# Expert stages of an attention and MoE kernel: a w2 remainder behind the group's end, two terms of a down tile amid the next, and another order of the next expert's preparation

## The chip, the cores and the metric

The kernel runs on one core of a Trainium2 chip. Its time is the device time of one execution in microseconds (us); the median of three runs of the kernel before is 734.19 us (733.92 to 736.5). The profile is that of one more execution, which took 734.46 us.

## The reference

The program computes causal attention with a decay for 8 batches of 8 heads, 576 rows and 64 values a head, and sends the result, as 4608 rows of 512 values, through a mixture of 8 experts with one expert a row:

```python
logits = x @ w_gate
expert_idx = np.argmax(logits, axis=1)
...
for e in range(E):
    mask = expert_idx == e
    xe = x[mask]
    h = np.maximum(xe @ w1[e], 0.0)
    ye = h @ w2[e]
    out[mask] = gate_w[mask, None] * ye
```

Here `w1[e]` is 512 x 1024 and `w2[e]` is 1024 x 512. The attention is not touched by the change.

## The kernel before

The attention and expert 0 take the first half of the span. From expert 1 on (the loop in `run` over `e`), each expert has an **up stage** and a **down stage**.

Every float32 factor is held as two parts: a high part, which ScalarE makes by a cast (`round_s`, `round_v`'s predecessor `split_v`, `split_t`), and a low part, the **remainder**, which VectorE or GpSimd makes as the factor less its high part. A product is then three matmuls: high by high, high by low, low by high.

**Up stage** (`sevens`, `group`, `product`). The expert's up to 640 rows are paired into 320 columns, and the product with w1 is done by Strassen's scheme: four groups of seven block products, 42 matmuls a group, 168 in all. A register picks one of three widths (320, 288 or 256 columns). The sums of input blocks are called T1 to T4; the unsummed input lies in `xa` and `B22`. The weight sums are made by GpSimd in four additions (`sums_s`, lines 1386 to 1389). After certain products ScalarE, VectorE and GpSimd combine the results (`after`, lines 1546 to 1569) and make h = Relu(...) in a high part `hh` (line 1538) and a low part `hl` (line 1541). GpSimd has one addition in it, `p5` (line 1560). The last steps of a group, `end`, a Relu and `last`, run amid the next group, and those of the last group at the head of the down stage (`self.ends`).

**Down stage** (`downs`, `down`). Five tiles of 128 rows, each the sum over eight hidden blocks of three matmuls (24 in all) with 512 columns into one PSUM bank. The blocks go in the order

```python
        terms = [(ft, *i) for ft in ((0, 1, 2, 4, 5, 6, 3, 7) if e else range(FT))
```

since blocks 3 and 7 come from the last group. Tiles 0, 2 and 4 use one PSUM bank, tiles 1 and 3 another. ScalarE then scales the tile into `y` (line 1293), and GpSimd scatters its rows into the output (line 1296). All of the fifth tile but its first matmul is skipped where an expert has few rows (`tail`).

**Weights.** w2 comes in four blocks `i` of two hidden blocks; block 3 holds hidden blocks 6 and 7. `split_v` casts a block (ScalarE, line 1416) and makes its remainder (VectorE, line 1417). w1 comes in four groups of two parts (`part` 0 of 128x1024 elements, `part` 1 of 128x768); line 1401 is the cast, line 1407 the remainder.

**Preparation of the next expert.** GpSimd gathers the rows of five input tiles (`fetch`), SP writes them to memory and reads them back in another order (`put`, `get`), VectorE transposes them into PSUM (`flip`, line 1178), and ScalarE and VectorE make the input sums from there (`turn_t`: copies at lines 1470 to 1472, six subtractions or additions at lines 1469 and 1476). `split_t` splits a finished sum T1 to T4 into its two parts (lines 1416 and 1417 again).

**What sets the order.** Two tables written by hand: `ups` says which preparation is issued after which of the 28 products (k = 0 to 27), `dns` which after which quarter of the first four down tiles (k = 0 to 15; four quarters a tile, two hidden blocks each). `InOrder.pin` ties every instruction to the one before it on its engine, so that the order of issue is the order in each engine's queue and in the DMA queues of SP and GpSimd. An engine whose next instruction waits holds up all behind it.

Of the kernel before, what the change touches and what calls it, by code (L numbers as in the profile page):

```python
# [9 lines left out]
F32 = mybir.dt.float32  # L10
# [5 lines left out]
ALU = mybir.AluOpType  # L16
# [6 lines left out]
S = 576  # L23
# [10 lines left out]
NST = CAP // P  # L34
# [4 lines left out]
FT = FF // P  # L39
# [1033 lines left out]
class Moe:  # L1073
# [185 lines left out]
    def down(self, e, m, part=(0, FT)):  # L1259

        c, nc = self.c, self.nc
        rows = self.rows_of_h(e, m)
        if part[0] == 0:
            self.py[m] = psum((c.ps_v, c.ps_m)[m % 2])
        py = self.py[m]
        terms = [(ft, *i) for ft in ((0, 1, 2, 4, 5, 6, 3, 7) if e else range(FT))
                 for i in ((0, 0), (0, 1), (1, 0))]

        def some(k0, k1):
            for k in range(k0, k1):  # L1270
                ft, hi_, wi = terms[k]
                c.note(nc.tensor.matmul(  # L1272
                    py, rows(hi_, ft), self.w2p[e, ft][wi],
                    start=k == 0, stop=k == len(terms) - 1, skip_group_check=tail,
                ))

        tail = e > 0 and m == NST - 1
        if tail:
            some(0, 1)
            few = self.tail  # L1280
            if e + 1 < E:
                self.begin_up(e + 1)
            else:
                self.tc.mark_branch_hint_location("overflow", engines=[mybir.EngineType.PE])
            with self.tc.If(few > 0):
                some(1, len(terms))
        else:
            some(3 * part[0], 3 * part[1])
        if part[1] < FT:
            return  # L1290
        _, si, g, s = self.index(e, m)
        y = c.yp.tile([P, D], F32, name="y")
        nc.scalar.activation(y, py, AF.Copy, scale=g[:, s : s + 1])  # L1293

        def scatter():
            nc.gpsimd.indirect_dma_start(  # L1296
                out=self.out,
                out_offset=bass.IndirectOffsetOnAxis(ap=si[:, s : s + 1], axis=0),
                in_=y, in_offset=None, bounds_check=self.x_dram.shape[0] - 1,
                oob_is_err=False,  # L1300
            )

        if tail and e + 1 < E:
            self.scatter = scatter
        else:
            scatter()
# [123 lines left out]

    def split_v(self, e, i):

        c = self.c
        hi, lo = (self.w2_part(c.words, i, k) for k in range(2))
        self.round(hi, lo, self.w2_part(c.values, i, 1))
        for f in range(2):
            self.w2p[e, 2 * i + f] = [w[:, f * D : f * D + D] for w in (hi, lo)]

# [164 lines left out]
    def run(self, run, tasks):  # L1603
        c, tc = self.c, self.tc
        T = lambda f, *args: lambda: f(*args)
# [3 lines left out]
        def downs(e, ms, tasks):  # L1609
            k = 0  # L1610
            for m in ms:
                for q in range(4):
                    if e and m == NST - 1:
                        if q == 0:
                            run(lambda: self.down(e, m))
                    else:
                        run(lambda: self.down(e, m, (2 * q, 2 * q + 2)))
                    for f in tasks.get(k, []):
                        run(f)
                    k += 1  # L1620

        with tc.tile_pool(name="moe_w2b", bufs=1, side="right") as w2b:
# [4 lines left out]
            S = lambda f, *args: T(f, 1, *args)  # L1627
# [20 lines left out]
        with tc.tile_pool(name="moe_h", bufs=1) as hp, tc.tile_pool(name="moe_u", bufs=1) as up_, \  # L1648
# [5 lines left out]
            for e in range(1, E):  # L1654
                self.h[e] = h
                if e == 1:
                    run(lambda: self.begin_up(e))
                S = lambda f, *args: T(f, e, *args)
                N = lambda f, *args: T(f, e + 1, *args)
                ups, dns = {}, {}  # L1660

                def at(d, *items):
                    for k, f in items:
                        d.setdefault(k, []).append(f)

                late = 9 if e == 1 else 1
                at(ups, (0, S(self.load_v, 0)), (0, S(self.load_v, 1)),
                   (4, S(self.round_s, 2, 1)), (6, S(self.rest_s, 2, 1, G)),
                   (late, S(self.load_v, 2)), (late, S(self.load_v, 3)),
                   (9 if e > 1 else 8, S(self.split_s, 3, 0)), (11, S(self.round_s, 3, 1)),  # L1670
                   (13, S(self.rest_s, 3, 1, G)))
                for i, k in enumerate((15, 22, 16, 23) if e == 1 else (10, 23, 16, 24)):
                    at(ups, (k, S(self.split_v, i)))
                if e == 1:
                    at(ups, (0, S(self.sums_s, 3)), (2, S(self.split_s, 2, 0)))
                else:
                    at(ups, (8, self.scatter))
                if e + 1 < E:
                    at(ups, (9, N(self.load_s, 0)), (16, N(self.load_s, 1)),
                       (6, fetch(e + 1, 3)), (6, fetch(e + 1, 4)), (13, fetch(e + 1, 2)),  # L1680
                       (15, fetch(e + 1, 0)), (19, fetch(e + 1, 1)), (20, N(self.sums_s, 0)),
                       (27, N(self.sums_s, 1)))
                    for m, i, k in ((3, 12, 16), (4, 13, 17), (2, 18, 22), (0, 21, 26), (1, 25, 27)):
                        at(ups, (i, N(self.put, m)), (k, N(self.get, m)))
                    at(dns, (0, N(self.begin_t)), (1, N(self.round_s, 0, 0)),
                       (2, N(self.round_s, 0, 1)), (5, N(self.flip, 3)), (5, N(self.flip, 4)),
                       (6, N(self.rest_s, 0, 0)), (6, N(self.turn_t, 3)),
                       (7, N(self.rest_s, 0, 1)), (7, N(self.load_s, 2)),
                       (7, N(self.turn_t, 4)), (9, N(self.flip, 2)), (9, N(self.split_s, 1, 0)),
                       (10, N(self.turn_t, 2)), (11, N(self.flip, 0)),  # L1690
                       (11, N(self.split_s, 1, 1)), (11, N(self.load_s, 3)),
                       (12, N(self.sums_s, 2)), (13, N(self.turn_t, 0)),
                       (14, N(self.flip, 1)), (15, N(self.turn_t, 1)),
                       (15, N(self.split_t, "T2")), (15, N(self.split_t, "T1")),
                       (15, N(self.split_t, "T4", G)), (15, N(self.split_t, "T3", G)),
                       (15, N(self.split_s, 2, 0)), (15, N(self.sums_s, 3)))
                else:
                    at(ups, (27, lambda: tc.keep_in_program_order(G.drain())))
                self.ends = [lambda: None] * 3
                self.sevens(e, run, ups)  # L1700
                dns.setdefault(0, [])[:0] = self.ends
                downs(e, range(NST), dns)


# [224 lines left out]
```

## Time and profile before

| what | value |
|---|---|
| median of 3 runs | 734.19 us (733.92 to 736.5) |
| the profiled execution | 734.46 us |
| its span, first to last instruction | 732.7 us |
| TensorE busy (matmuls) | 719.4 us, 98% |
| VectorE busy | 559.2 us, 76% |
| GpSimd busy | 549.5 us, 75% |
| ScalarE busy | 496.7 us, 68% |
| mean granted TensorE clock | 0.986 of full speed |

The profile names TensorE's matmuls PE, its weight loads PEld, VectorE DVE, ScalarE ACT, GpSimd POOL and SyncE SP. A row names line, engine, operation and tile. "Idle before" is the time for which the engine stood idle ahead of an instruction, with what ended the wait. The end of a matmul is modelled, so the pace of TensorE is read from start to start. Times in the rows are counted from the start of the span.

### The profile page before, as it was taken

The numbers are of one execution on the slowest core, as the hardware profiler recorded it, in microseconds if no ns is written. First come the engines' busy times: TensorE is split into PE (matmuls) and PEld (weight loads), VectorE is DVE, ScalarE is ACT, GpSimd is POOL, SyncE is SP. The second block draws the span as 40 slices with busy tenths as digits, with TensorE's granted clock in tenths as the row PEclk, the third lists the DMA queues.
The fourth block names the chain that finished last, engine by engine and source line by source line (L and its number), as shares of the span: only waits on it lengthen the run. The fifth ranks groups of instructions, "written<-read, shape, count | busy, mean of one in ns | idle before, by whom it ended". The sixth has DMA issues, their size and how long they took to land.

```text
span 732.7 us, 18458 instructions
## 1 busy us (share of the span) xinstructions
PE 719.4 (98%) x6321; PEld 620.6 (85%) x6321; DVE 559.2 (76%) x1614; ACT 496.7 (68%) x1319; POOL 549.5 (75%) x696
## 2 busy tenths in 40 slices
PE   9999999999999999999999999999999999999997
PEld 4888888888888888798898898897898887998985
DVE  6678898989898988671979777798698697796830
ACT  6999999999999999352665555574565664755631
POOL 5999989898989888945687497595794794884711
PEclk8999999999999999899999999999999999999999
DMA  6886788867776756324357376384574574673301
GB/s 181 210 193 178 193 208 205 211 187 219 194 212 192 214 190 226 109 95 132 112 191 239 123 235 202 118 262 154 187 208 147 170 230 133 194 220 99 126 22 42
DMA packets 98724, 127.59 MB, mean 174 GB/s; under 512 B 10287, under 2 KB 56367, under 8 KB 98608
## 3 DMA queue, kind: packets, MB, share of 16 engines
q1 hardware_dynamic: 91568, 106.12, 49.4%
q0 software_dynamic: 6400, 19.93, 8.3%
q8 instruction: 71, 1.16, 0.7%
q14 instruction: 45, 0.37, 0.2%
q10 hardware_dynamic: 640, 0.01, 0.0%
HBM read 99.12 MB, written 27.93 MB: 173 GB/s over the span
## 4 chain that ended last, share of the span: by engine, by line
PE 75%; POOL 11%; issue 5%; DVE 4%; DMA 4%; ACT 1%; POOLq 0%; DVEq 0%; ACTq 0%
PE ps L1272 24%; PE ps L1492 12%; PE ps L526 11%; PE ps L403 9%; PE ps L455 7%; PE ps L437 4%; PE ps L1227 3%; PE ps L450 2%; POOL w L1090 1%; POOL xg L1156 1%; DMA bias<-ud 1%; PE ps L617 1%; POOL w1r L1387 1%; PE pr L1492 1%; POOL X_1w L1417 1%
## 5 line engine op out<-in xcount | busy, mean ns | idle before, releaser
L422 ACT ACTIVATE sc<-sc,nmx 128x512 f32<-128x512 f32 (+3 forms) x256 | 142.3, 558 | 5.3 <-DVE nmx L379 4.1
L1296 POOL DMA_INDIRECT out<-y,si_fast x40 | 44.2, 1105 | 90.5 <-ACT y L1293 73.5
L1272 PE MATMUL ps<-w_0w,hhw 128*128 128x512 f32 x273 | 106.5, 390 | 2.1 <-ACT hhw L1538 2.1
L1492 PE MATMUL ps<-X_0w,w1s 128*128 128x320 f32 (+2 forms) x504 | 107.6, 304 | 0.0
L1272 PE MATMUL ps<-w_0w,hl 128*128 128x512 f32 x272 | 107.5, 395 | 0.0
L1272 PE MATMUL ps<-w_1w,hhw 128*128 128x512 f32 x272 | 106.7, 392 | 0.0
L467 ACT COPY aT<-ps 128x512 f32<-128x512 f32 (+1 forms) x224 | 93.3, 506 | 1.3 <-PE ps L455 0.3
L330 POOL TENSOR_TENSOR hl<-raw,hl 128x640 fp32r<-128x640 f32 (+1 forms) x60 | 89.6, 1493 | 5.0
L526 PE MATMUL ps<-aT,va_t 128*64 128x256 f32 (+3 forms) x896 | 90.6, 354 | 0.0
L1293 ACT ACTIVATE y<-ps,g_fast 128x512 f32<-128x512 f32 x40 | 27.5, 687 | 85.5 <-PE ps L1272 62.7
L1492 PEld LDWEIGHTS ps<-X_0w,w1s 128*128 128x128 f32 x504 | 83.1, 190 | 0.1
L526 PEld LDWEIGHTS ps<-aT,va_t 128*64 128x64 f32 x896 | 56.4, 137 | 28.7 <-issue 5.4
L403 PE MATMUL ps<-hl 64*128 64x512 f32 (+1 forms) x720 | 80.5, 340 | 0.0
L1492 PE MATMUL ps<-X_1w,w1s 128*128 128x320 f32 (+2 forms) x252 | 76.2, 302 | 0.0
L379 DVE CUSTOM_DVE_ANT_0 sc<-ps,bias 128x128 f32<-128x128 f32 (+1 forms) x128 | 59.8, 486 | 10.1 <-PE ps L403 4.6
L1272 PEld LDWEIGHTS ps<-w_0w,hhw 128*128 128x128 f32 x273 | 51.3, 188 | 14.3 <-ACT hhw L1538 3.4
L1272 PEld LDWEIGHTS ps<-w_1w,hhw 128*128 128x128 f32 x272 | 51.1, 188 | 11.5
L1272 PEld LDWEIGHTS ps<-w_0w,hl 128*128 128x128 f32 x272 | 51.1, 188 | 11.2 <-DVE hl L1541 0.9
L379 DVE CUSTOM_DVE_ANT_1 sc<-ps,bias 128x256 f32<-128x256 f32 (+1 forms) x128 | 57.7, 487 | 3.6 <-PE ps L403 3.5
L1492 PE MATMUL ps<-xa,w1s 128*128 128x320 f32 (+2 forms) x336 | 56.8, 304 | 3.4 <-ACT xa L1472 1.2
L1407 DVE TENSOR_TENSOR w1s<-w1r,w1s 128x1024 fp32r<-128x1024 f32 (+1 forms) x42 | 49.6, 1183 | 10.8 <-ACT w1s L1401 10.7
L403 PEld LDWEIGHTS ps<-hl 64*128 64x128 f32 x720 | 52.4, 185 | 3.3
(252 smaller groups left out, 1896.5 us busy)
## 6 DMA issues: line engine op xcount, KB each, us to landing
bias<-ud SPq DMA_DIRECT2D x30, 576.0 KB, 5.8
w1r<-in_w SPq DMA_DIRECT2D x112, 128.0 KB, 2.6
w<-in_w SPq DMA_DIRECT2D x28, 512.0 KB, 5.5
raw<-in_qkT SPq DMA_DIRECT2D x64, 160.0 KB, 3.4
raw<-in_qkT SPq DMA_DIRECT2D x64, 144.0 KB, 3.7
va_t<-in_va SPq DMA_DIRECT2D x32, 256.0 KB, 5.7
x_dram<-row SPq DMA_DIRECT2D x32, 256.0 KB, 2.7
xs<-xg SPq DMA_DIRECT2D x30, 256.0 KB, 3.6
```

What stands on the lines that cost most here:

```text
L330: return eng.tensor_tensor(hl[:, 1], raws[n][:, r : r + w], hl[:, 0].bitcast(F32), ALU.subtract)
L379: red_last[:] = [V.tensor_tensor_reduce(dst, src, in1, -0.125, init, ALU.add, ALU.min, nms[n][:, col : col + 1]).ins]
L403: note(nc.tensor.matmul(pb[j][:, o : o + w], q[js], k[js], start=(i == 0), stop=(i == len(terms) - 1),))
L422: A.activation(x, x, AF.Exp, bias=nms[n][:, 5 * j + t : 5 * j + t + 1], scale=-1.0, accum_out=ssums[b][:, t, 2 * p + j : 2 * p + j + 1])
L437: note(nc.tensor.matmul(pb[half][:, 0:JW], q, k, start=(i == 0), stop=(i == len(terms) - 1),))
L455: note(nc.tensor.transpose(out.bitcast(F32R), words, c.identr[rows, rows]))
L467: copy_on = {"a": lambda o, i: A.copy(o, i), "v": lambda o, i: V.tensor_copy(o, i)}
L526: note(nc.tensor.matmul(pv[j * HD : (j + 1) * HD, q0 - qa : qb - qa], l, r, start=(blk == 0), stop=(blk == nb - 1),))
L1272: c.note(nc.tensor.matmul(py, rows(hi_, ft), self.w2p[e, ft][wi], start=k == 0, stop=k == len(terms) - 1, skip_group_check=tail,))
L1296: nc.gpsimd.indirect_dma_start(out=self.out, out_offset=bass.IndirectOffsetOnAxis(ap=si[:, s : s + 1], axis=0), in_=y, in_offset=None, bou ...
L1407: (eng or self.nc.vector).tensor_tensor(lo, raw, hi.bitcast(F32), ALU.subtract)
L1492: self.nc.tensor.matmul(bank[:, 0:cols], w[:, wi, mat, kt], x[xi][:, kt, 0:cols], start=start and k == 0, stop=k == 5, skip_group_check=True,)
```

## The change

Four edits, all in experts 1 to 7.

1. `split_v` is cut into `round_v` (the cast) and `rest_v` (the remainder). For w2 block 3 the cast stays after product 23 or 24, and the remainder goes behind the three last steps of the last product group, at the head of the down stage.
2. In the first down tile (`head`), the two terms that use that remainder, (6, 0, 1) and (7, 0, 1), are sorted to the end, held back, and issued by `finish_down` after the first quarter of the second tile, with the tile's scaling and scatter (now `down_out`) behind them.
3. In `dns` the casts, transposes, input tiles and splits of the next expert stand at other quarters, most of them earlier: the last input tile is turned at 10 instead of 15, the sums T1 to T4 are split at 12 and 14 instead of 15.
4. The remainders of both parts of w1 group 0 and of part 1 of group 1 go from VectorE to GpSimd (argument `G`); those of T3 and T4 go from GpSimd to VectorE.

```diff
--- before.py
+++ after.py
@@ -1265,16 +1265,18 @@
         py = self.py[m]
         terms = [(ft, *i) for ft in ((0, 1, 2, 4, 5, 6, 3, 7) if e else range(FT))
                  for i in ((0, 0), (0, 1), (1, 0))]
+        tail, head = (e > 0 and m == t for t in (NST - 1, 0))
+        if head:
+            terms.sort(key=lambda t: t in ((6, 0, 1), (7, 0, 1)))
 
         def some(k0, k1):
             for k in range(k0, k1):
                 ft, hi_, wi = terms[k]
                 c.note(nc.tensor.matmul(
                     py, rows(hi_, ft), self.w2p[e, ft][wi],
-                    start=k == 0, stop=k == len(terms) - 1, skip_group_check=tail,
+                    start=k == 0, stop=k == len(terms) - 1, skip_group_check=tail or head,
                 ))
 
-        tail = e > 0 and m == NST - 1
         if tail:
             some(0, 1)
             few = self.tail
@@ -1285,9 +1287,17 @@
             with self.tc.If(few > 0):
                 some(1, len(terms))
         else:
-            some(3 * part[0], 3 * part[1])
+            some(3 * part[0], 3 * part[1] - (2 if head and part[1] == FT else 0))
         if part[1] < FT:
             return
+        if head:
+            self.finish_down = lambda: (some(len(terms) - 2, len(terms)), self.down_out(e, m, py, tail))
+        else:
+            self.down_out(e, m, py, tail)
+
+    def down_out(self, e, m, py, tail):
+
+        c, nc = self.c, self.nc
         _, si, g, s = self.index(e, m)
         y = c.yp.tile([P, D], F32, name="y")
         nc.scalar.activation(y, py, AF.Copy, scale=g[:, s : s + 1])
@@ -1430,9 +1440,20 @@
 
     def split_v(self, e, i):
 
+        self.round_v(e, i)
+        self.rest_v(i)
+
+    def rest_v(self, i):
+
+        hi, lo = (self.w2_part(self.c.words, i, k) for k in range(2))
+        self.nc.vector.tensor_tensor(lo, self.w2_part(self.c.values, i, 1), hi.bitcast(F32),
+                                     ALU.subtract)
+
+    def round_v(self, e, i):
+
         c = self.c
         hi, lo = (self.w2_part(c.words, i, k) for k in range(2))
-        self.round(hi, lo, self.w2_part(c.values, i, 1))
+        self.nc.scalar.copy(hi, self.w2_part(c.values, i, 1))
         for f in range(2):
             self.w2p[e, 2 * i + f] = [w[:, f * D : f * D + D] for w in (hi, lo)]
 
@@ -1615,6 +1636,8 @@
                             run(lambda: self.down(e, m))
                     else:
                         run(lambda: self.down(e, m, (2 * q, 2 * q + 2)))
+                        if e and (m, q) == (1, 0):
+                            run(self.finish_down)
                     for f in tasks.get(k, []):
                         run(f)
                     k += 1
@@ -1669,8 +1692,9 @@
                    (late, S(self.load_v, 2)), (late, S(self.load_v, 3)),
                    (9 if e > 1 else 8, S(self.split_s, 3, 0)), (11, S(self.round_s, 3, 1)),
                    (13, S(self.rest_s, 3, 1, G)))
-                for i, k in enumerate((15, 22, 16, 23) if e == 1 else (10, 23, 16, 24)):
+                for i, k in enumerate((15, 22, 16) if e == 1 else (10, 23, 16)):
                     at(ups, (k, S(self.split_v, i)))
+                at(ups, (23 if e == 1 else 24, S(self.round_v, 3)))
                 if e == 1:
                     at(ups, (0, S(self.sums_s, 3)), (2, S(self.split_s, 2, 0)))
                 else:
@@ -1683,22 +1707,23 @@
                     for m, i, k in ((3, 12, 16), (4, 13, 17), (2, 18, 22), (0, 21, 26), (1, 25, 27)):
                         at(ups, (i, N(self.put, m)), (k, N(self.get, m)))
                     at(dns, (0, N(self.begin_t)), (1, N(self.round_s, 0, 0)),
-                       (2, N(self.round_s, 0, 1)), (5, N(self.flip, 3)), (5, N(self.flip, 4)),
-                       (6, N(self.rest_s, 0, 0)), (6, N(self.turn_t, 3)),
-                       (7, N(self.rest_s, 0, 1)), (7, N(self.load_s, 2)),
-                       (7, N(self.turn_t, 4)), (9, N(self.flip, 2)), (9, N(self.split_s, 1, 0)),
-                       (10, N(self.turn_t, 2)), (11, N(self.flip, 0)),
-                       (11, N(self.split_s, 1, 1)), (11, N(self.load_s, 3)),
-                       (12, N(self.sums_s, 2)), (13, N(self.turn_t, 0)),
-                       (14, N(self.flip, 1)), (15, N(self.turn_t, 1)),
-                       (15, N(self.split_t, "T2")), (15, N(self.split_t, "T1")),
-                       (15, N(self.split_t, "T4", G)), (15, N(self.split_t, "T3", G)),
-                       (15, N(self.split_s, 2, 0)), (15, N(self.sums_s, 3)))
+                       (1, N(self.round_s, 0, 1)), (2, N(self.flip, 3)), (2, N(self.flip, 4)),
+                       (2, N(self.turn_t, 3)), (2, N(self.turn_t, 4)),
+                       (2, N(self.rest_s, 0, 0, G)), (2, N(self.rest_s, 0, 1, G)),
+                       (6, N(self.flip, 2)), (6, N(self.flip, 0)), (6, N(self.turn_t, 2)),
+                       (7, N(self.turn_t, 0)), (7, N(self.load_s, 2)),
+                       (7, N(self.split_s, 1, 0)), (8, N(self.round_s, 1, 1)),
+                       (8, N(self.rest_s, 1, 1, G)), (8, N(self.flip, 1)),
+                       (10, N(self.turn_t, 1)), (11, N(self.load_s, 3)),
+                       (12, N(self.split_t, "T2")), (12, N(self.split_t, "T1")),
+                       (12, N(self.sums_s, 2)), (14, N(self.split_t, "T4")),
+                       (14, N(self.split_t, "T3")), (15, N(self.split_s, 2, 0)),
+                       (15, N(self.sums_s, 3)))
                 else:
                     at(ups, (27, lambda: tc.keep_in_program_order(G.drain())))
                 self.ends = [lambda: None] * 3
                 self.sevens(e, run, ups)
-                dns.setdefault(0, [])[:0] = self.ends
+                dns.setdefault(0, [])[:0] = [*self.ends, T(self.rest_v, 3)]
                 downs(e, range(NST), dns)
```

## Rows read from the trace of the kernel before

**Rows 1.** By stage: us, busy PE, PEld, DVE, ACT, POOL (instructions); clock, DMA, GB/s.

```profile
391.85:420.05 28.20, 27.94 (x122) 22.39 (x121) 22.43 (x49) 13.60 (x31) 15.96 (x17) 1.00 0.49 158
420.05:444.69 24.64, 24.64 (x169) 24.64 (x168) 18.54 (x31) 15.50 (x30) 23.05 (x20) 1.00 0.76 244
444.69:472.19 27.50, 27.50 (x123) 22.55 (x122) 22.07 (x49) 13.61 (x31) 14.79 (x16) 1.00 0.39 128
...
494.64:523.26 28.62, 27.92 (x123) 22.38 (x121) 22.87 (x50) 13.93 (x32) 16.38 (x17) 1.00 0.43 135
...
597.22:622.37 25.15, 22.82 (x100) 17.88 (x98) 20.25 (x43) 11.34 (x28) 15.26 (x16) 1.00 0.53 165
622.37:649.80 27.43, 26.41 (x168) 26.15 (x169) 22.51 (x39) 18.76 (x34) 23.52 (x21) 0.94 0.71 218
```

**Rows 2.** Waits of TensorE, 367 to 727 us: us, times, longest.

```profile
PE ps L1272 <- ACT hhw L1538: 2.1, 3, 1.1
...
PE ps L1492 <- ACT w1s L1401: 1.1, 1, 1.1
```

**Rows 3.** Timeline of TensorE, expert 5, tile 0: start, us, what, idle before.

```profile
601.11 0.40 PE L1272 MATMUL ps<-w_0w,hl 128*128 128x512 f32 x1
602.64 0.50 PE L1272 MATMUL ps<-w_0w,hhw 128*128 128x512 f32 x1 [1.13 <-ACT hhw L1538]
```

**Rows 4.** Timeline of the other engines, 596.6 to 604.6 us, expert 5.

```profile
596.69 2.91 DVE L1417 TENSOR_TENSOR w_1w<-w,w_0w 128x1024 fp32r<-128x1024 f32 x2
...
598.48 1.72 POOL L1388 TENSOR_TENSOR w1r<-w1r 128x256 f32<-128x256 f32 x1
600.17 0.73 POOL L1389 TENSOR_TENSOR w1r<-w1r 128x256 f32<-128x256 f32 x1
...
600.86 0.87 POOL L1560 TENSOR_TENSOR u<-u,u 128x320 f32<-128x320 f32 x1
...
602.16 0.43 ACT L1538 ACTIVATE hhw<-ps 128x320 fp32r<-128x320 f32 x1
...
602.71 0.48 DVE L1541 SCALAR_TENSOR_TENSOR hl<-ps,hhw 128x320 fp32r<-128x320 f32 x1
```

**Rows 5.** Timeline of TensorE, expert 5 to expert 6.

```profile
620.78 0.39 PE L1272 MATMUL ps<-w_0w,hhw 128*128 128x512 f32 x1
622.37 0.56 PE L1492 MATMUL ps<-xa,w1s 128*128 128x320 f32 x2 [1.20 <-ACT xa L1472]
623.94 1.44 PE L1492 MATMUL ps<-xa,w1s 128*128 128x320 f32 x4 [1.01 <-DVE xa L1469]
```

**Rows 6.** Timeline of ScalarE and VectorE at the same place.

```profile
619.77 1.09 DVE L1178 STREAM_TRANSPOSE ps<-xg 128x512 f32<-128x512 f32 x1
...
621.03 0.69 ACT L1293 ACTIVATE y<-ps,g_fast 128x512 f32<-128x512 f32 x1 [2.86 <-issue]
...
621.61 0.26 ACT L1470 COPY X<-ps 128x128 f32<-128x128 f32 x1
...
622.35 0.29 DVE L1469 TENSOR_TENSOR X<-ps,X 128x128 f32<-128x128 f32 x1 [1.48 <-ACT xa L1472]
...
623.47 0.42 DVE L1469 TENSOR_TENSOR xa<-ps,xa 128x256 fp32r<-128x256 f32 x1
```

**Rows 7.** Groups by shape on VectorE, 391.85 to 677.3 us: busy us, mean ns.

```profile
L1407 DVE TENSOR_TENSOR w1s<-w1r,w1s 128x1024 fp32r<-128x1024 f32 x22 | 26.7, 1215 | 7.7 <-ACT w1s L1401 7.7
...
L1417 DVE TENSOR_TENSOR X_1w<-X,X_0w 128x640 fp32r<-128x640 f32 x12 | 9.4, 822 | 0.8
```

**Rows 8.** Groups by shape on GpSimd, the same stretch.

```profile
L1417 POOL TENSOR_TENSOR X_1w<-X,X_0w 128x640 fp32r<-128x640 f32 x11 | 22.7, 2078 | 14.1 <-ACT X_0w L1416 14.1
...
L1407 POOL TENSOR_TENSOR w1s<-w1r,w1s 128x768 fp32r<-128x768 f32 x10 | 18.7, 1866 | 0.0
```

**Rows 9.** SP's last reads back, expert 5; DMA issues, 590:612, us to landing.

```profile
602.34 3.07 SPq L1171 DMA_DIRECT2D xg<-xs  x2
...
xg<-xs SPq DMA_DIRECT2D x5, 256.0 KB, 4.2
```

## The prediction

> **What bounds the kernel now.** First the page: TensorE is busy for nearly the whole span and the matmuls are the same before and after, so only time in which TensorE waits or runs slowly can be won, and only from the first expert's end on, where the edits lie. Second, a table by stage, one stretch per up or down stage [rows 1]. An undisturbed down stage of five tiles (120 matmuls) takes 27.50 us, 0.229 us a matmul and 5.50 us a tile. The same work takes 28.20 us in expert 1 and 28.62 us in expert 3: 0.70 and 1.12 us over. Expert 5 skips its fifth tile after one matmul (97 in all), which should be 97 x 0.229 = 22.23 us, and takes 25.15: 2.92 over. The up stage behind it, of full width as the undisturbed one of 24.64 us, takes 27.43: 2.79 over, at a mean granted clock of 0.94 where the other five have 1.00. These four sums, 7.53 us or 1.0% of the span, are all that the edits aim at.
>
> Third, who ended the waits: a Relu on ScalarE in the down stage (2.1 us in three places), and one wait of 1.1 us in the middle of expert 5's up stage, put down to a ScalarE cast [rows 2]. I leave that last one as it is: the work that it is put down to keeps its place in the change.
>
> **The stall inside tile 0.** The down products go through the 1024 hidden columns in the order 0, 1, 2, 4, 5, 6, 3, 7, because blocks 3 and 7 come from the last product group. In expert 5 the first matmul of block 3 starts at 602.64 us where the pace gives 601.11 + 0.23 = 601.34: 1.30 us late [rows 3]. It needs the Relu that ends at 602.16 + 0.43 = 602.59. Walk back [rows 4]: that Relu stands behind another which waited for a GpSimd addition (600.86 to 601.73), which stood behind GpSimd's four weight sums. The third of these took 1.72 us, the fourth 0.73. Beside the third VectorE was making the remainders of two w2 blocks, 2.91 us for the pair, where a remainder of 128x1024 has a mean of 1.22 elsewhere [rows 7]: each engine holds up the other. VectorE's own part of that addition also stood behind the pair.
>
> **The change, part by part.**
> *Last w2 remainder behind the group's end.* One 128x1024 subtraction leaves this place in each of seven experts. The VectorE chain comes forward by 2.91 - 1.22 = 1.7 us. GpSimd's third sum should fall from 1.72 to about 0.73, so its addition ends 0.99 earlier, at 600.74. GpSimd is the later of the two, so the gain is 0.99, not 1.7. The two Relus then end at 602.59 - 0.99 = 601.60.
> *Two terms of tile 0 put last.* Block 6's remainder term leaves the place ahead of block 3, so block 3 is wanted one matmul earlier, at 601.11 in expert 5. What is left there: 601.65 - 601.11 = 0.54 us, and the smaller delays behind it (1.56 in all less 1.30 = 0.26, where 1.56 is 2.92 less the 1.36 before the next stage, below): 0.80. By the same shift (-0.99 + 0.23 = -0.76) expert 3 keeps some 0.36 of its 1.12 and expert 1 nothing of its 0.70. I round expert 3's rest down to 0.2, since part of its 1.12 are the small delays after the stall. So 0.70 + 1.12 + 1.56 = 3.38 us becomes 1.0: **2.4 us won**. Bounds: 0 (the sums don't get shorter) and 3.38.
> *The deferred terms themselves.* They run after 28 other matmuls, 28 x 0.229 = 6.4 us into the stage, at 603.6 + 0.8 = 604.4 in expert 5. VectorE's last remainder of the group now ends at 602.71 + 0.48 = 603.19 [rows 4], then at 602.20; the w2 remainder behind it takes 1.22 to 1.7 and is there by 603.9. No stall; cover 0.5 us.
> *Tile 0's output later.* Its ScalarE evacuation (0.69 us, [rows 6]) now waits for 30 matmuls, and stands behind the copies of two input tiles, which wait for two VectorE transposes (1.09 each) behind the w2 remainder: 603.9 + 2.2 + 0.7 (copies, 621.61 to 622.35) + 0.7 = 607.5. Its PSUM bank is wanted by tile 2 at 597.22 + 0.8 + 48 x 0.229 = 609.0. Spare 1.5 us; cost nothing. Its scatter queues behind GpSimd's remainders, and its buffer is wanted again only by tile 2's output.
> *GpSimd makes three remainders.* One of 128x1024 and two of 128x768 per expert: 1.87 us each for the small [rows 8], an estimated 1.87 x 1024/768 = 2.5 for the large, 6.2 in all. It gives up two 128x640 remainders of 2.08. VectorE loses 3.2 us and gains 2 x 0.82. None of these is wanted by TensorE before the next up stage, 20 us on. SP's loads of the third weight group wait for the first two remainders: GpSimd is through its four sums at 600.74 + 4 x 0.73 = 603.7 and with both remainders at 608.1; before, VectorE had them behind transposes and an input tile at 603.19 + 2 x 1.09 + 1.22 = 606.6 and, 1.54 and some 1 later, 609.1. That queue is no later. The bounds are 0 and what the second rival says.
> *Input tiles earlier.* This is the other large term. In expert 5 TensorE goes from its last down matmul at 620.78 to the first up matmul at 622.37, then waits again until 623.94 [rows 5]: the last input tile is transposed only at 619.77, and its copies stand on ScalarE behind tile 3's output at 621.03, which ends with that tile; the low part of the input is there at 623.89 [rows 6]. Everywhere else the fifth tile covers this. In the new order ScalarE copies the last input tile before tile 2's output. VectorE's queue from 603.9: two transposes, two tiles of six subtractions (1.54 each, 622.35 to 623.89), two transposes, two tiles, one weight remainder, transpose, tile: 603.9 + 5 x 1.09 + 5 x 1.54 + 1.22 = 618.3. The re-read rows were issued by 605.41 and take 4.2 us to land [rows 9], so they are there before their transposes. The splits of the four input sums follow, a cast and a remainder of 0.82 [rows 7] each: the first by 618.3 + 2 x 0.82 = 619.9, the fourth by 622.4. The up products start at 620.2 and come 24.64/28 = 0.88 us apart, and the second, third, fourth and sixth want these sums: 621.1 to 624.6. In time by 1.2 us or more.
> So 1.59 - 0.23 = 1.36 us goes before the stage, and its 2.79 over: 4.15. In that 2.79 are 1.2 us of the second wait and some 1.5 of a clock at the lower level: 0.94 over 27.43 us is 0.06/0.5 x 27.43 = 3.3 us at 1.2 instead of 2.4 GHz, and it came right after these two waits; the waits of 1.1 to 1.3 us elsewhere brought no lower clock. What stays is the jump over the skipped tile, which no other stage shows: between 0 and 1.36; I take 0.3, as a stage change without a jump shows none. **3.85 us won**.
> *Sum.* The profiled execution took 734.46 us (span 732.7 and 1.8 around it), 0.27 above the median of 734.19. 734.46 - 2.4 - 3.85 = 728.2, less 0.27: **727.9 us**, 0.86% faster.
>
> **A rule of the Trainium skill.** [Rows 4] show the two engines lengthening each other. "SBUF — State Buffer", section "SBUF: two separate sides", says why: a VectorE instruction with two SBUF inputs and a GpSimd instruction exclude each other for the whole instruction, it is a lock and no sharing. The pair at 2.91 and the sum at 1.72 agree with it. By that rule the longer GpSimd remainders speak against this change: each may hold a VectorE remainder for its whole length. The third rival below is that outcome.
>
> **Rivals.**
> 1. *Only the input tiles help.* GpSimd's sums stay long, because the remaining w2 remainder and the chain before them set their end; tile 0 stalls as now or by 0.23 more in three experts. For: GpSimd has hardly a gap through the up stage. Against: the fourth sum, with no remainder beside it, took 0.73. Time: 734.46 - 3.85 + 0.5 - 0.27 = 730.8; if half comes through, 729.6. Chance 0.13.
> 2. *Only tile 0 helps.* The splits of the input sums run beside GpSimd's sums for the third group and take up to twice as long, or the jump and tile 4's output cost as much as the wait now does. For: the margins of little over 1 us above. Against: the first products want only the input itself. Time: 734.46 - 2.4 - 0.27 = 731.8. Chance 0.15.
> 3. *Slower: tile 0's output blocks tile 2.* If a GpSimd remainder gets ahead of VectorE's w2 remainder, it holds that, and behind it the transposes, the copies and the evacuation at 607.5, by up to 2.5 us, or 4.4 with the second. Six experts pay what exceeds 1.5 us: with 4.4 it is 6 x 2.9 = 17 us, 745; it turns to a loss from 6.25/6 = 1.04 us beyond the spare, a hold of 2.5. Against: GpSimd's sums last until 603.7 and the w2 remainder asks at 602.2. Chance 0.07.
> 4. *It does neither*, since another wait takes over in both places: 734.2, chance 0.05.
>
> **Chances.** The forecast has 0.60, with its own range from 726.6 (all 7.53 won) to 729.5. This kernel can tell about 0.5%, 3.7 us, from no change: faster is below 730.5, which takes the forecast, half of rival 1 and a little of 2, where the first wait goes whole: 0.70. The same has 0.21: the rest of 1 and 2, and 4. Slower has 0.09: rival 3 and something not seen. The range goes from 725.8 (with the wait of 1.1 us in expert 5's up stage gone too) to 732.2, which takes in rivals 1 and 2.
>
> **What would show it.** Right: expert 3's and 5's first block 3 matmul late by under 0.6 us; the third sum before it near 0.73; no gap over 0.5 us between expert 5's last down and first up matmul, and a granted clock of 1.00 in that up stage; tile 0's evacuation done by 10.5 us into the stage. Wrong: a wait of TensorE at a tile 2, at the deferred terms, or for an input sum's split; GpSimd's sums still at 1.7.

## The result and the profile after

The changed kernel took 726.88 us (median of six runs, 725.69 to 728.06), the kernel before 733.87 us in the same rounds (six runs, 731.74 to 736.5): a ratio of 0.9912 [0.9893, 0.9932]. The forecast was 727.9 us, a ratio of 0.9914. The profiled execution took 727.32 us with a span of 725.5, against 734.46 and 732.7 before.

The table by stage again, from the first product of a stage to the first of the next. Columns as in [rows 1]; the rows are expert 1's, 2's, 3's and 5's down stage and the up stage behind expert 5.

```profile
390.87:418.37 27.50, 27.50 (x122) 22.50 (x121) 23.20 (x49) 14.20 (x31) 22.18 (x19) 1.00 0.52 153
...
443.01:470.51 27.50, 27.50 (x122) 22.54 (x121) 23.30 (x48) 14.19 (x31) 23.01 (x20) 1.00 0.39 126
492.97:520.82 27.85, 27.85 (x122) 22.38 (x121) 23.44 (x50) 14.50 (x32) 23.28 (x19) 1.00 0.40 125
594.05:617.85 23.80, 22.84 (x99) 17.89 (x98) 21.41 (x48) 14.00 (x32) 19.02 (x16) 1.00 0.56 178
617.85:642.60 24.75, 24.75 (x169) 24.74 (x169) 21.03 (x33) 16.23 (x31) 22.98 (x21) 1.00 0.72 221
```

Beside [rows 1], expert 1 lost the whole of its 0.70 us, expert 3 kept 0.35 of 1.12, expert 5 kept 1.57 of 2.92, and the up stage behind it came down from 27.43 to 24.75 at a full granted clock. POOL's busy time in these down stages rose by 3.8 to 8.2 us: it has the remainders now. Two of TensorE's four waits from 360 us to the end matter here (us in total, times, longest); the Relu's three waits of [rows 2] are one, and the second is the jump over the skipped tile. The other two, of 0.4 and 0.3 us, lie in the up stages of experts 1 and 5:

```profile
PE ps L1275 <- ACT hhw L1559: 0.6, 1, 0.6
...
PE ps L1513 <- PEq L1287: 0.3, 1, 0.3
```

TensorE at the two places of [rows 3] and [rows 5], in expert 5 (start, us, what, idle before): block 3's first product, and the step to expert 6.

```profile
597.52 0.39 PE L1275 MATMUL ps<-w_0w,hhw 128*128 128x512 f32 x1
...
598.79 0.50 PE L1275 MATMUL ps<-w_0w,hhw 128*128 128x512 f32 x1 [0.64 <-ACT hhw L1559]
...
617.14 0.39 PE L1275 MATMUL ps<-w_0w,hhw 128*128 128x512 f32 x1
617.85 0.84 PE L1513 MATMUL ps<-xa,w1s 128*128 128x320 f32 x4 [0.32 <-PEq L1287]
```

Tile 0 now waits at 597.52 + 2 x 0.23 = 597.98 and goes on at 598.79: 0.81 us instead of 1.30. The step to the next expert has 617.85 - 617.14 = 0.71 us between two starts that are 0.23 apart elsewhere: 0.48 lost, and no second wait. GpSimd around tile 0:

```profile
595.62 0.74 POOL L1398 TENSOR_TENSOR w1r<-w1r 128x256 f32<-128x256 f32 x1
596.32 0.74 POOL L1399 TENSOR_TENSOR w1r<-w1r 128x256 f32<-128x256 f32 x1
597.01 0.87 POOL L1581 TENSOR_TENSOR u<-u,u 128x320 f32<-128x320 f32 x1
...
599.50 1.73 POOL L1398 TENSOR_TENSOR w1r<-w1r 128x256 f32<-128x256 f32 x1
...
601.88 4.22 POOL L1417 TENSOR_TENSOR w1s<-w1r,w1s 128x1024 fp32r<-128x1024 f32 x2
```

The third sum of the old group takes 0.74 us instead of the 1.72 of [rows 4]; the same instruction of the next group (599.50) takes 1.73, because the moved w2 remainder (599.25, below) now lies beside it, where no product waits for the sum. ScalarE and VectorE in the same stage:

```profile
598.31 0.42 ACT L1559 ACTIVATE hhw<-ps 128x320 fp32r<-128x320 f32 x1
...
603.25 0.72 ACT L1303 ACTIVATE y<-ps,g_fast 128x512 f32<-128x512 f32 x1
...
612.85 0.39 ACT L1493 CAST xa<-ps 128x256 fp32r<-128x256 f32 x1
613.12 0.71 ACT L1303 ACTIVATE y<-ps,g_fast 128x512 f32<-128x512 f32 x1
```

```profile
599.25 1.37 DVE L1449 TENSOR_TENSOR w_1w<-w,w_0w 128x1024 fp32r<-128x1024 f32 x1
...
614.40 0.42 DVE L1490 TENSOR_TENSOR xa<-ps,xa 128x256 fp32r<-128x256 f32 x1
614.95 4.44 DVE L1427 TENSOR_TENSOR X_1w<-X,X_0w 128x640 fp32r<-128x640 f32 x4
```

Tile 0's output leaves at 603.97, 9.9 us into the stage. The last input tile's copies stand ahead of tile 2's output. Its low part is there at 614.82, 20.8 us into the stage instead of 26.7 (623.89 in [rows 6]), and VectorE's splits of the input sums begin 2.9 us before the next stage's first product.

### The profile page after: what moved, and what is told of

Its sections match the earlier page's. It is cut to its first block, busy times and chain, and to the rows that moved or that the text cites. A ratio compares the mean times of both kernels' runs of the same rounds, so it can differ in the third digit from the quotient of the medians.

```text
span 725.5 us, 18440 instructions
## 1 busy us (share of the span) xinstructions
PE 715.7 (99%) x6321; PEld 617.2 (85%) x6321; DVE 555.9 (77%) x1608; ACT 497.9 (69%) x1319; POOL 573.7 (79%) x702
## 5 line engine op out<-in xcount | busy, mean ns | idle before, releaser
L1306 POOL DMA_INDIRECT out<-y,si_fast x40 | 48.1, 1202 | 59.5 <-ACT y L1303 27.9
L1417 POOL TENSOR_TENSOR w1s<-w1r,w1s 128x768 fp32r<-128x768 f32 (+1 forms) x32 | 62.8, 1968 | 0.1
```

The lines of the kernel that those rows point to most:

```text
L1306: nc.gpsimd.indirect_dma_start(out=self.out, out_offset=bass.IndirectOffsetOnAxis(ap=si[:, s : s + 1], axis=0), in_=y, in_offset=None, bou ...
L1417: (eng or self.nc.vector).tensor_tensor(lo, raw, hi.bitcast(F32), ALU.subtract)
```

## The experiments

**The unchanged kernel again.** Is what I account for a property of the kernel or of one execution?

> The kernel before, unchanged, profiled once more. Theory: the stalls of the expert stages belong to the program and come again within 0.2 us each: 0.70 and 1.12 us over 27.50 in the down stages of experts 1 and 3, 2.92 over in expert 5, 2.79 over in the up stage of expert 6. What lies outside them does not: the low clock near 300 us (which cost 1.6 us there) and the 1.3 us in the middle of expert 5's up stage. Rival: those two come again as well and the change removed them.

One run, 731.91 us. TensorE's waits from 367 us on:

```profile
PE ps L1272 <- ACT hhw L1538: 2.4, 3, 1.4
PE ps L1492 <- ACT xa L1472: 1.2, 1, 1.2
PE ps L1492 <- DVE xa L1469: 1.0, 1, 1.0
```

The four stages came to 28.23, 28.64, 25.42 and 27.56 us, within 0.27 of [rows 1]; the 0.27 is in expert 5's down stage, over the 0.2 that I had expected. The stretch of lower clock near 300 us, in code that the change does not touch, did not come again, and the mid-stage wait of expert 5's up stage shrank from 1.1 to under 0.2. So the two big terms belong to the kernel. Of the 7.2 us between the first two spans, 1.6 lie ahead of expert 1's up stage and do not belong to the change; that stage itself took 0.6 us more in the changed kernel's execution (25.36 against 24.76), and 24.97 and 24.93 in two later ones.

**One half alone.** The w2 remainder and tile 0's order on the kernel before (`x2`), and the table of down-stage chores on the kernel before (`x3`).

`x2` takes over, with the deferral that goes with them, these lines:

```diff
+        if head:
+            terms.sort(key=lambda t: t in ((6, 0, 1), (7, 0, 1)))
...
+                at(ups, (23 if e == 1 else 24, S(self.round_v, 3)))
...
+                dns.setdefault(0, [])[:0] = [*self.ends, T(self.rest_v, 3)]
```

`x3` takes over the new table of chores, with GpSimd's remainders in it:

```diff
+                       (2, N(self.rest_s, 0, 0, G)), (2, N(self.rest_s, 0, 1, G)),
...
+                       (8, N(self.rest_s, 1, 1, G)), (8, N(self.flip, 1)),
```

> The kernel before with the w2 remainder behind the group's end and the deferred terms only; the order of the preparation and the engines of the remainders as before. Theory (the terms of the sum add): the stalls in tile 0 of experts 1, 3, 5 fall from 3.38 to 1.43 us, as in the changed kernel, and the gap into expert 6 stays: 1.95 us faster, 731.9 us for a before of 733.9; GpSimd's third sum before expert 5's tile 0 takes 0.74 us. Rival: without the new order VectorE has no room and the deferred terms or tile 2 wait; then no gain or a loss of a few us.

> The kernel before with the new order of the preparation and the three remainders on GpSimd only; the w2 remainder stays before the group's end, no deferred terms. Theory: the gap into expert 6 shrinks from 1.36 + 2.79 us over to 0.5 + 0.1 and its clock stays at the upper level: 3.6 us faster, 730.3 us; the stalls in tile 0 stay at 0.7, 1.1 and 1.5 to 1.6 us. Rival: the new order needs the w2 remainder out of the way, and its transposes come too late: under 2 us faster.

By stages, expert 1's down and the up stage behind expert 5; first `x2`, then `x3`:

```profile
389.54:417.06 27.52, 27.52 (x122) 22.52 (x121) 22.02 (x49) 13.61 (x31) 15.55 (x17) 1.00 0.51 159
...
617.88:645.53 27.65, 26.63 (x169) 26.29 (x169) 22.18 (x39) 18.47 (x34) 23.71 (x21) 0.94 0.69 215
```

```profile
390.79:419.00 28.21, 27.93 (x122) 22.38 (x121) 23.02 (x49) 14.28 (x31) 22.30 (x21) 1.00 0.49 151
...
620.02:644.74 24.72, 24.72 (x168) 24.72 (x169) 19.63 (x32) 15.96 (x31) 22.96 (x21) 1.00 0.77 229
```

| us | down 1 | down 3 | up 5 | down 5 | up 6 | against the kernel before |
|---|---|---|---|---|---|---|
| before, second execution | 28.23 | 28.64 | 21.58 | 25.42 | 27.56 | |
| `x2` | 27.52 | 27.85 | 21.57 | 24.66 | 27.65 | 730.66, 0.9968 [0.9952, 0.9984] |
| `x3` | 28.21 | 28.63 | 21.09 | 24.59 | 24.72 | 728.47, 0.9936 [0.9915, 0.9957] |
| changed kernel | 27.50 | 27.85 | 21.09 | 23.80 | 24.75 | 726.88, 0.9912 [0.9893, 0.9932] |

Each half takes away its own term and leaves the other's. Against the second execution, `x2` wins 2.2 us in these stages, `x3` 4.2 and the whole change 6.4: the halves add up by stages. The whole time cannot show that: in two later sets of rounds the changed kernel stood at 0.9936 and 0.9933, where `x3` alone stands. The lower clock in the up stage belongs to the two waits ahead of it: with them (`x2`) the stage has a mean of 0.94, without them (`x3`) 1.00.

**The w2 remainder late, but wanted on time.** The terms keep their old order, so tile 0 waits for the moved remainder.

```diff
-        tail, head = (e > 0 and m == t for t in (NST - 1, 0))
+        tail, head = e > 0 and m == NST - 1, False
...
-                        if e and (m, q) == (1, 0):
-                            run(self.finish_down)
```

> The changed kernel without the deferred terms: the w2 remainder stays behind the group's end, tile 0 runs its 24 matmuls in the old order. Theory: block 6's remainder term is wanted 16 x 0.229 = 3.67 us into the down stage, and the remainder ends at 5.5, 4.5, 5.8, 4.5, 6.6, 5.2 and 3.7 us in experts 1 to 7, so TensorE waits 1.8, 0.8, 2.2, 0.8, 2.9, 1.5 and 0 us: 10.0 in all, which takes the place of the 1.4 in tile 0 now: 8.6 us slower than the changed kernel, 735.5, more if the clock falls after the long waits. Rival: the remainder alone would have been in time or nearly so, and the deferral is worth under 2 us.

736.83 us, 1.005 [1.0032, 1.0069] of the kernel before. The wait, and expert 1's, 3's and 5's down stages:

```profile
PE ps L1275 <- DVE w_1w L1449: 8.5, 6, 2.8
```

```profile
390.28:419.71 29.43, 27.79 (x122) 22.46 (x121) 23.68 (x49) 14.17 (x32) 23.39 (x21) 1.00 0.51 151
...
495.29:526.71 31.42, 29.38 (x123) 23.61 (x122) 23.91 (x50) 14.57 (x32) 25.16 (x21) 0.95 0.39 120
600.86:628.07 27.21, 24.12 (x99) 19.02 (x98) 22.68 (x49) 14.21 (x32) 21.37 (x18) 0.94 0.48 158
```

Moving the remainder without deferring the products that need it loses more than the whole change wins: all six experts wait, and the two longest waits (2.2 and 2.9 us) brought a lower clock on top. The deferral is what makes the move free.

**The terms last in tile 0, but not amid the next tile.**

```diff
-            some(3 * part[0], 3 * part[1] - (2 if head and part[1] == FT else 0))
+            some(3 * part[0], 3 * part[1])
...
-                        if e and (m, q) == (1, 0):
-                            run(self.finish_down)
```

> The changed kernel with the two terms at the end of tile 0, but not held back into tile 1. Theory: they are wanted 22 x 0.229 = 5.04 us into the stage plus the stall ahead of them (0.35 in expert 3, 1.08 in expert 5), and the remainder ends at 5.5, 4.5, 5.8, 4.5, 6.6, 5.2 and 3.7 us: waits of 0.45, 0, 0.45, 0, 0.45, 0.15 and 0, in all 1.5 us slower than the changed kernel. Rival (sorting them last was all that was needed): no difference.

```profile
PE ps L1275 <- DVE w_1w L1446: 0.9, 3, 0.3
```

Expert 1, 3 and 5 took 28.04, 28.45 and 24.40 us, 1.7 more in all than the changed kernel. In total time, 728.06 us, 0.994 [0.9927, 0.9953], it cannot be told from the changed kernel run beside it (728.05, 0.9936 [0.9916, 0.9957]), whose stages repeated within 0.03 us:

> The changed kernel once more, on the chip of the three others and in the same rounds, as their measure. Theory: the stage times come again within 0.1 us (27.50, 27.50, 27.85, 27.50, 23.80, 27.50 for the down stages), and what differs from run to run lies in the attention and in the two up stages that show small waits.

**Where the rest of tile 0's stall comes from.** GpSimd's sums for the next group queue after the up stage instead of amid it.

```diff
-                       (15, fetch(e + 1, 0)), (19, fetch(e + 1, 1)), (20, N(self.sums_s, 0)),
+                       (15, fetch(e + 1, 0)), (19, fetch(e + 1, 1)), (27, N(self.sums_s, 0)),
```

> The changed kernel with GpSimd's four sums for the next expert's first weight group moved from product 20 to product 27, behind its addition for the last product group. Theory (what is left of the stall in tile 0 is GpSimd's queue ahead of that addition): in expert 5 the addition then runs as soon as VectorE's sum is there, 1.4 us into the stage, the Relu ends at 3.2 where 3.9 is wanted, and the 0.35 us in expert 3 and 1.1 in expert 5 go: 1.4 us faster than the changed kernel. Rival: the sums come back later as a wait of ScalarE's cast, of the input tiles' copies and of tile 0's output; then no gain.

Expert 5's down stage, the up stage behind it, and there TensorE and ScalarE:

```profile
593.05:615.77 22.72, 22.40 (x99) 18.04 (x98) 20.79 (x48) 13.97 (x32) 16.98 (x15) 1.00 0.51 165
615.77:643.13 27.36, 24.99 (x169) 24.74 (x170) 20.45 (x34) 16.14 (x31) 20.99 (x22) 1.00 0.74 230
```

```profile
618.36 0.31 PE L1513 MATMUL ps<-X_1w,w1s 128*128 128x320 f32 x1
621.03 0.56 PE L1513 MATMUL ps<-X_0w,w1s 128*128 128x320 f32 x2 [2.36 <-ACT y L1303]
```

```profile
618.21 1.05 ACT L1411 CAST w1s<-w1r 128x1024 fp32r<-128x1024 f32 x1 [2.26 <-POOL w1r L1397]
620.29 0.69 ACT L1303 ACTIVATE y<-ps,g_fast 128x512 f32<-128x512 f32 x1 [1.03 <-DMA out<-y,si_fast]
```

Expert 3 and 5 fell to 27.51 and 22.72 us, which is 97 x 0.229 and the jump: GpSimd's sums were the whole of the rest. But in this execution the up stage behind took 27.36 us instead of 24.75. Tile 4's output stands on ScalarE behind a weight cast that waited 2.26 us for GpSimd's sums, then waits another 1.03 us for an earlier scatter to land, and the next up stage wants that output's bank: a wait of 2.4 us there. The theory had only the gain, and the rival had looked for the late sums at other places. In total time, 726.38 us, 0.9913 [0.9899, 0.9926], it cannot be told from the changed kernel beside it (728.05, 0.9936); the profiled execution, 727.78, is the slowest of the five, so whether the wait comes each time is not shown.

So the next kernel also moves that cast behind the output (`x9`):

```diff
-                    at(ups, (8, self.scatter))
+                    at(ups, (2, S(self.split_s, 2, 0)), (8, self.scatter))
...
-                       (15, fetch(e + 1, 0)), (19, fetch(e + 1, 1)), (20, N(self.sums_s, 0)),
+                       (15, fetch(e + 1, 0)), (19, fetch(e + 1, 1)), (27, N(self.sums_s, 0)),
...
-                       (14, N(self.split_t, "T3")), (15, N(self.split_s, 2, 0)),
-                       (15, N(self.sums_s, 3)))
+                       (14, N(self.split_t, "T3")), (15, N(self.sums_s, 3)))
```

> The kernel of x5_sums_late, with the cast and the remainder of the first part of w1 group 2 moved from the end of the down stage to product 2 of the next up stage. In x5 the 1.4 us won in tile 0 were given back by one wait of 2.5 us in expert 6's up stage: the fourth product wants tile 4's PSUM bank, tile 4's output stood on ScalarE behind that cast, and the cast waited for GpSimd's sums, which had become later. Theory: with the cast behind the output the wait goes, expert 6's up stage takes 24.7 us again, the down stages 27.5 and 22.7: 1.4 us faster than the changed kernel. Rival: the cast, or GpSimd's late sums, hold up another step of that up stage (it is wanted at product 14), and the gain is given back again.

> The changed kernel again, as the measure of the other two in the same rounds: stage times within 0.1 us of those seen twice.

```profile
594.39:617.11 22.72, 22.40 (x99) 18.05 (x98) 20.78 (x48) 13.92 (x32) 17.08 (x16) 1.00 0.47 148
617.11:642.20 25.09, 25.09 (x169) 24.75 (x169) 21.38 (x32) 15.88 (x31) 21.21 (x20) 1.00 0.75 230
```

The 2.4 us wait is gone and 25.09 is left of 27.36. How much of it the cast made and how much the scatter's landing, this does not separate. By stages the kernel is some 1.1 us below the changed one; in time, 726.27 us, 0.9918 [0.9898, 0.9937], it cannot be told from it (726.68, 0.9933 [0.9912, 0.9955]).

**GpSimd's three remainders back to VectorE** (`x6`).

```diff
-                       (2, N(self.rest_s, 0, 0, G)), (2, N(self.rest_s, 0, 1, G)),
+                       (2, N(self.rest_s, 0, 0)), (2, N(self.rest_s, 0, 1)),
...
-                       (8, N(self.rest_s, 1, 1, G)), (8, N(self.flip, 1)),
+                       (8, N(self.rest_s, 1, 1)), (8, N(self.flip, 1)),
```

> The changed kernel with the three w1 remainders made by VectorE again, at the same places. Theory (the new order is what pays; GpSimd only gives room): VectorE's queue before the last input tile grows by 1.22 + 2 x 0.95 = 3.1 us; the last tile's splits in expert 5 end at 619 to 622 where the up products want them from 618.9 to 622.4, and tile 2's output ends at 21.5 to 22.1 us into a stage where tile 4 wants its bank at 22.0: 0 to 1 us slower than the changed kernel. Rival: VectorE becomes the bound of the down stage, each of experts 1 to 6 waits at tile 4 and expert 6's first products wait again: over 2 us slower.

731.36 us, 0.9989 [0.9975, 1.0003], where the changed kernel beside it had 728.05, 0.9936: most of the gain is gone, though TensorE waits for none of these remainders. By stages 4.9 us are lost. Expert 1's stage took 28.46 us, expert 3's 28.86, expert 6's 28.03 and the up stage behind expert 5 26.35. In expert 1, ScalarE and then TensorE where tile 4 begins:

```profile
410.18 0.27 ACT L1491 COPY X<-ps 128x128 f32<-128x128 f32 x1 [3.27 <-DVE ps L1178]
...
410.77 0.71 ACT L1303 ACTIVATE y<-ps,g_fast 128x512 f32<-128x512 f32 x1
```

```profile
412.02 0.39 PE L1275 MATMUL ps<-w_0w,hhw 128*128 128x512 f32 x1
413.06 0.50 PE L1275 MATMUL ps<-w_1w,hhw 128*128 128x512 f32 x1 [0.66 <-issue]
```

VectorE is later by the remainders, so its last input tile is, so ScalarE's copies are, and tile 2's output behind them ends at 411.48, when tile 4 is about to take its bank. Tile 4 begins with one product and then a branch on whether the tile is skipped. That first product starts on the pace (412.02), so the wait of 0.1 to 0.2 us for the bank, which the next expectation speaks of, is not there, nor in experts 3 and 6. What is lost lies behind it: 1.04 us between two products instead of 0.23, and in them the trace has the sequencer's register load and branch, from 411.94 to 413.01. I read this as the sequencer held up by the late output. The test is to let the output go ahead of the copies (`x11`, on `x6`):

```diff
-                       (10, N(self.turn_t, 1)), (11, N(self.load_s, 3)),
+                       (11, N(self.turn_t, 1)), (11, N(self.load_s, 3)),
```

> The kernel of x6_no_gpsimd_remainders, with the last input tile turned at quarter 11, behind tile 2's output on ScalarE, instead of at 10. In x6 tile 4's first matmul waited 0.1 to 0.2 us for its bank in experts 1, 3 and 6, and TensorE then stood 0.4 to 0.9 us more, in which its sequencer loaded a register and branched. Theory: tile 2's output stood behind the copies of the last input tile, whose transpose VectorE reached 3 us later; with the output ahead of them the down stages of experts 1, 3 and 6 fall from 28.5, 28.9 and 28.0 to 27.5, 27.9 and 27.5, and most of expert 5's and 6's excess goes with it, since GpSimd's scatter and sums come earlier: 4 of the 4.9 us that x6 lost come back. Rival: VectorE's longer queue is itself the bound; the waits stay in place.

```profile
408.50 0.71 ACT L1303 ACTIVATE y<-ps,g_fast 128x512 f32<-128x512 f32 x1
...
411.89 0.27 ACT L1491 COPY X<-ps 128x128 f32<-128x128 f32 x1 [2.68 <-DVE ps L1178]
```

729.4 us, 0.9957 [0.994, 0.9974]. Expert 1, 3 and 6 are back at 27.54, 27.86 and 27.50 us, and by stages 3.6 of the 4.9 us have come back. What stays is mostly the next up stage at 25.94: TensorE waits 0.7 us there for the bank of an output and 0.4 for the cast of an input sum. In total time the kernel is still above the changed one beside it (726.68, 0.9933). So GpSimd's remainders pay by letting the last input tile be early, not by what they compute.

## Why the prediction was right, step by step

- **What bounds it.** Right: the four stages hold the gain, with expert 5's up stage, below. Every other stage of experts 2 to 6 stayed within 0.01 us; expert 1's up stage took between 24.76 and 25.36 us in the two kernels' executions.
- **The w2 remainder and tile 0's order: 2.4 us forecast.** Against the profiled execution before, 3.38 us of stalls came down to 0.35 + 1.09 = 1.44 (1.09 is 23.80 less 22.23 and the jump's 0.48), so 1.9 was won. The mechanism is right, by the sum that fell from 1.72 to 0.74 us and by `x2`. Two sizes are off. Expert 3 kept the 0.36 that the sum gave and I had rounded down to 0.2. Expert 5's first wait is 0.81 and not 0.54, nor under the 0.6 that I had named as the sign. The step of 0.76 us was right there, and the base that I took it from was not: block 3 is 1.30 us late in the profiled execution, but 1.58 in the second one of the same kernel (599.87 where the pace gives 598.29) and 1.57 in `x3`. In the profiled execution TensorE had itself come later, by the odd wait in expert 5's up stage. `x2`, with that up stage at 21.57, is late by 0.81 as the changed kernel is with 21.09.

```profile
599.87 0.50 PE L1272 MATMUL ps<-w_0w,hhw 128*128 128x512 f32 x1 [1.41 <-ACT hhw L1538]
```

- **The wait left as it is.** That was wrong: the wait of 1.1 us in expert 5's up stage went. The three profiled executions with the old table of chores (the kernel before twice, and `x2`) took 21.83, 21.58 and 21.57 us there, the ten with the new table 21.06 to 21.09. So it goes with the table, and not with the three remainders that GpSimd got: `x6` has 21.08 without them. Nor is it the cast that the profile names: in `x2` and in the second execution the same product starts before that cast ends. What held that product for 1.3 us in the first execution, 0.5 in `x2` and 0.1 in the second stays open, but the stage is 0.5 us longer in all three. The traces show a way, GpSimd and VectorE, in the second execution first and then in the changed kernel:

```profile
571.66 4.20 POOL L1417 TENSOR_TENSOR X_1w<-X,X_0w 128x640 fp32r<-128x640 f32 x2 [2.35 <-ACT X_0w L1416]
...
579.55 1.86 POOL L1407 TENSOR_TENSOR w1s<-w1r,w1s 128x768 fp32r<-128x768 f32 x1
...
580.30 1.45 DVE L1541 SCALAR_TENSOR_TENSOR hl<-u,hhw 128x320 fp32r<-128x320 f32 x1
```

```profile
579.04 1.87 POOL L1417 TENSOR_TENSOR w1s<-w1r,w1s 128x768 fp32r<-128x768 f32 x1
...
580.67 0.59 DVE L1562 SCALAR_TENSOR_TENSOR hl<-u,hhw 128x320 fp32r<-128x320 f32 x1
```

With the old table GpSimd made the remainders of T4 and T3 at the head of this up stage, and so its sums and the weight remainder behind them came later: 7.0 us into the stage instead of 6.1. There that remainder lies beside VectorE's low part of h, 7.7 us into the stage in both, and this takes 1.45 us instead of 0.59. VectorE is then 0.5 us late for a later product's bank. So the step that failed is "the work that it is put down to keeps its place": what was ahead of it on GpSimd did not. No run moves T3's and T4's remainders alone, so this is read from the traces and not tested.

- **The deferred terms and tile 0's output.** Right: no wait at either. The remainder ends at 600.62, 6.6 us into the stage, where the forecast had the terms at 604.4 - 597.22 = 7.2; the output leaves 9.9 us into it, where tile 2 was forecast to want the bank at 11.8. `x4` prices the deferral at 736.83 less 728.05 or 726.88, about 9 us, in different rounds.
- **GpSimd's remainders.** Costing nothing was right, and TensorE waits for no remainder of GpSimd's. What I did not see is that the input tiles need them (`x6`), so this edit and the next are one.
- **The input tiles: 3.85 us forecast.** 4.15 came down to 0.48 + 0.11, so 3.56. The one size that is off is the jump: 0.48 us and not 0.3. The last input tile was there at 614.82 where I had 618.3 in a stage that began 3.17 us later: the offset into the stage is 20.8 and 21.1.
- **The sum.** 1.9 + 3.6 = 5.5, with the up stage's 0.7 it is 6.2 us; the forecast had 6.25. That the total fits this closely is luck: two misses, of 0.5 and 0.3 us, met a wait of 0.7 that the forecast had left alone. The measured difference of medians, 7.0 us (5.0 to 7.9 by the ratio's interval), holds it; in the two later sets of rounds it was 4.7 and 5.9 us. The low end of the range, 725.8, does not come out of its own terms, 734.46 - 0.27 - 7.53 - 1.1 = 725.6; nothing rests on it.
- **The rivals.** Rivals 1 and 2 fall by `x2` and `x3`: each half helps, and they add up. Rival 3 did not happen, but its kind did, where an output stands behind another chore on ScalarE: `x5` (2.4 us in the profiled execution) and `x6` (3.6 us by stages, which `x11` gave back).

**The rule on the lock.** The moved remainder and GpSimd's sum beside it took 1.37 and 1.73 us, the splits of the input sums 0.82 to 1.68, the long ones beside GpSimd's sums of 1.21 and 1.32. This is what the Trainium skill, "SBUF — State Buffer", section "SBUF: two separate sides", says of a VectorE instruction with two SBUF inputs and a GpSimd instruction that reads SBUF: one holds up the other for its whole length. The change does not avoid the lock, it moves it to where nobody waits.

## What to carry to other kernels

A chore that stands on an in-order engine just ahead of the last link of a stage is paid by TensorE, even where that engine has room on the average; put it behind the link, and put the products that need it last, or the move costs more than it gives (`x4`). Before taking work off or moving it, look at what stands behind it on the engine that evacuates the outputs: in three of these kernels (`x5`, `x6`, `x11`) TensorE waited for the bank of an output and not for the moved work. Read such changes by stage: the down stages of the changed kernel repeated within 0.03 us in three executions, where the whole time scatters by more than the last microsecond that is to be won. Take the base from more than one execution: the stalls of the kernel before differed by up to 0.3 us between two.

## What the runs showed of the hardware

- Where TensorE branches over the skipped tile and nothing else waits, 0.48 us are lost (617.14 to 617.85, and the same 0.71 in `x4`, `x5` and `x7` to `x10`). Where it takes the tile but its sequencer gets to the register load and branch only then, some 0.8 us (`x6`, 412.02 to 413.06); in the changed kernel nothing is lost at that place.
- The lower clock (1.2 instead of 2.4 GHz) came after single waits of 2.2 and 2.9 us in `x4` and after 1.2 and 1.0 us in close order in `x2`, but not after 2.4 us in `x5`. A wait's length alone does not tell.
- In the early part, which is the same in all, a stretch of lower clock near 300 us came in some executions and not in others of the same code (the first, not the second of the kernel before), and lies in the part that makes 1.6 us of the difference between the first two traces. One profiled execution beside another is not good for less than that, unless it is read by stage.
